# Gate scores of a dense mixture: tokens as the stationary operand of 96 small matmuls, and column sums in columns that the products leave free

## The chip, the cores and the metric

The kernel runs on one core of one Trainium2 chip. The metric is the device time of one execution in microseconds (us). The engines of a core work side by side, each through its own list of instructions, and wait for each other by semaphores: TensorE (PE, with its weight loads shown as PEld), VectorE (DVE), ScalarE (ACT), GpSimd (POOL) and SyncE (SP), which issues most of the transfers (DMA).

## The reference, cut to what matters

Three stages follow one another: a decayed linear attention, a mixture of experts that sends each of the N = 1536 tokens to one of 8 experts, and a second, dense mixture in which every token passes all 8 experts. The change lies in the gate of the dense mixture:

```
logits = x @ w_gate                  # x: 1536 x 512, w_gate: 512 x 8
logits = logits - logits.max()       # one maximum over all tokens and experts
P = np.exp(logits)
for _ in range(8):
    P /= P.sum(1, keepdims=True) + 1e-09
    P /= P.sum(0, keepdims=True) + 1e-09
    P *= N / E
for e in range(E):
    out += P[:, e:e+1] * (np.maximum(x @ w1[e], 0.0) @ w2[e])
```

## The kernel before, in words

All matrix products of the two mixtures keep float32 accuracy by splitting an operand into a high and a low part of the type float32r: `x2T[0]` and `x2T[1]` hold the two parts of the transposed tokens of the dense mixture, `w1r` and `w2r`/`w2l` those of the weights, `hb` those of the hidden values. The helper `product` multiplies hi by hi, hi by lo and lo by hi: 12 matmuls of 384 columns for one 128 x 384 block of hidden values (lines 780 to 782 of the profile). `relu` then reads the block out of PSUM, first on ACT (L785), then on DVE (L786).

PSUM has eight banks of 512 columns. Banks 0 to 5 collect the output of six blocks of 128 tokens. Banks 6 and 7, called `pa` and `pc`, take the products in turn; a product uses columns 0 to 383 of its bank.

The dense mixture goes through its work in groups, and the order of the instructions is written out by hand. Group 0 is `opening`: four products (z = 0 to 3) with nothing between them. It stands in both branches of a condition on the number of slots of the first mixture, so the instructions behind it come after a branch. Groups 1 to 3 are run by `eight(n, points)`: for each z a product, its `relu`, and three `triple`s (three matmuls of 512 columns each, L969 to L971) that use the hidden values of the group before. `points` names small functions that are called at the end of a given z of a given group. Group 4 and most later ones are run by `seven`.

The gate of the dense mixture is spread over this order. `dense_gate` writes the gate weights to `wg2s`, 8 columns of high parts and 8 of low parts; the other 112 of 128 columns hold zeros (memset, L442). Behind the branch, before group 1, come on ACT and DVE the last weight splits of the opening's expert: `conv1(7, NE)`, whose transfer of the second weights SP may issue only when the split has read the buffer, and `conv2(4)` to `conv2(7)`, of which the last needs that transfer (L297 on ACT, L298 on DVE). On PE, `gate_scores(c)` for c = 0 to 2 takes `wg2s` as the stationary operand and 512 tokens as the moving one: 24 matmuls into banks 0 to 2 (L817). ACT copies the 16 rows that matter into `lgT`, a view of the tile `snap` (L818). Then

- group 1, z = 0: `gate_exp` turns the scores and folds the two halves together with 12 float32 matmuls of 8 columns, each of which runs as two instructions (L823), and DVE copies them to `Pm` and takes a maximum (L824, L825);
- group 1, z = 1: `gate_peak`, one small matmul (L829) that waits for that maximum;
- group 1, z = 2: `gate_shift`, another small matmul (L834), the exponential and the first sums over rows;
- groups 2 and 3, each z: `balance(at)`, a matmul of `Pm` with ones (L849, 96 columns, two instructions) into columns 0 to 95 of the bank of that z, then eight short operations on DVE (L850 to L853 and L840 to L843), the last of which gives the `Pm` that the next balance needs.

POOL adds up blocks of `x2T` into `snap` for the later groups (`xwhole`, L866 to L875) and splits them (`xsplit`, L880), beginning with group 1.

Of the kernel before, what the change touches and what calls it, by code (L numbers as in the profile page):

```python
# [11 lines left out]
F32 = mybir.dt.float32  # L12
F32R = mybir.dt.float32r
BF16 = mybir.dt.bfloat16
I32 = mybir.dt.int32
AF = mybir.ActivationFunctionType
ALU = mybir.AluOpType
AX = mybir.AxisListType
# [3 lines left out]
C = 128  # L22
# [4 lines left out]
NE = 8  # L27
# [89 lines left out]
def build(tc, i, out):  # L117
# [3 lines left out]
    with ctx:  # L121
# [13 lines left out]
        onesb = base.tile([128, 128], BF16, name="onesb")  # L135
        trib = base.tile([128, 128], BF16, name="trib")
        wg2f = base.tile([128, 4, NE], F32, name="wg2f")
        wg2s = base.tile([128, 4, 128], F32R, name="wg2s")
        mb = base.tile([128, 2, NE], F32, name="mb")
        midr = base.tile([128, M, 2], I32, name="midr")  # L140
        midf = base.tile([128, M], F32, name="midf")
# [260 lines left out]
        def attention_and_routing():  # L402
            with ExitStack() as st:
# [35 lines left out]
                V.memset(zero, 0.0)  # L439
                V.memset(onesb, 1.0)  # L440
                V.memset(ohsum, 0.0)
                V.memset(wg2s.bitcast(F32), 0.0)  # L442
                V.tensor_scalar(out=flip, in0=k("iota"), scalar1=k("phi"), scalar2=None, op0=ALU.is_equal)
                for h in range(2):
                    for g in range(4):
# [199 lines left out]
        with ExitStack() as st2:  # L645
# [138 lines left out]
            def relu(h, src):  # L784
                A.activation(out=h[:, 0], in_=src, func=AF.Relu)  # L785
                V.scalar_tensor_tensor(out=h[:, 1], in0=src, scalar=0.0, in1=h[:, 0].bitcast(F32), op0=ALU.max, op1=ALU.subtract)  # L786
# [3 lines left out]
            def opening():  # L790
                for z in range(4):
                    fi, th = z % 2, z // 2
                    b = (pa, pc)[z % 2][:, 0:HT]
                    product(b, lambda t, kk: w1b[fi][:, t, kk], lambda t, kk: x2T[t][:, kk, th * HT:(th + 1) * HT], True, True, 4)
                    relu(hs[0][fi][th], b)

            with tc.If(nsv < NREST + 1) as short:
                opening()
# [8 lines left out]
            sraw = op.tile([128, 4, 256], F32, name="sraw")  # L807
            snap = op.tile([128, 4, HT], F32, name="snap")
            oacc = []
            lgT = snap.rearrange("p u t -> p (u t)")[0:2 * NE]  # L810
            rs, cs, gm = tab[:, 430:430 + M], tab[:, 446:446 + NE], tab[:, 458:460]
            ones12 = [128, M, NE]
            def gate_scores(c):
                b = bank[c]
                for t in range(2):
                    for kk in range(4):
                        T.matmul(out=b, lhsT=wg2s[:, kk], rhs=x2T[t][:, kk, c * 512:(c + 1) * 512], start=t == 0 and kk == 0, stop=t == 1 and kk == 3)  # L817
                A.activation(out=lgT[:, c * 512:(c + 1) * 512], in_=b[0:2 * NE], func=AF.Copy)  # L818

            def gate_exp():  # L820
                b = bank[5]
                for m in range(M):
                    T.matmul(out=b[:, m * NE:(m + 1) * NE], lhsT=lgT[:, m * C:(m + 1) * C], rhs=k("fold")[0:2 * NE], start=True, stop=True)  # L823
                V.tensor_copy(out=Pm, in_=b[:, 0:M * NE].rearrange("p (m e) -> p m e", e=NE))  # L824
                V.tensor_reduce(out=gm[:, 0:1], in_=Pm, axis=AX.XY, op=ALU.max)  # L825

            def gate_peak():
                b = bank[5][:, 128:256]
                T.matmul(out=b[0:1, 0:128], lhsT=gm[:, 0:1], rhs=gtab[:, 0, 0:128], start=True, stop=True)  # L829
                V.tensor_reduce(out=gm[0:1, 1:2], in_=b[0:1, 0:128], axis=AX.X, op=ALU.max)  # L830

            def gate_shift():
                b = bank[5][:, 256:257]
                T.matmul(out=b[:, 0:1], lhsT=ones[0:1], rhs=gm[0:1, 1:2], start=True, stop=True)  # L834
                V.tensor_scalar(out=Pm, in0=Pm, scalar1=b[:, 0:1], scalar2=None, op0=ALU.subtract)
                A.activation(out=Pm, in_=Pm, func=AF.Exp)
                balance_rows()
# [7 lines left out]
            left = [ITERS]  # L845

            def balance(at):
                b = at[:, 0:M * NE]
                T.matmul(out=b, lhsT=ones, rhs=Pm.rearrange("p m e -> p (m e)"), start=True, stop=True)  # L849
                V.tensor_reduce(out=cs, in_=b.rearrange("p (m e) -> p e m", e=NE), axis=AX.X, op=ALU.add)  # L850
                V.tensor_scalar(out=cs, in0=cs, scalar1=1e-9, scalar2=None, op0=ALU.add)
                V.reciprocal(out=cs, in_=cs)
                V.scalar_tensor_tensor(out=Pm, in0=Pm, scalar=float(N) / NE, in1=bc(cs, 1, ones12), op0=ALU.mult, op1=ALU.mult)  # L853
                left[0] -= 1
                if left[0]:
                    balance_rows()
# [122 lines left out]
            def eight(n, points):  # L979
# [9 lines left out]
                for z, (fi, th) in enumerate(((0, 0), (1, 0), (0, 1), (1, 1))):  # L989
# [1 line left out]
                    h = hs[n][fi][th] = spare.pop(0)  # L991
                    product(b, w[fi], lambda t, kk, th=th: x2T[t][:, kk, (2 * p + th) * HT:(2 * p + th + 1) * HT], True, True, 4)
                    relu(h, b)
                    for _ in range(3):
                        for fn in (next(todo, None),):
                            if fn:
                                fn()
                    if old and z in (1, 3):
                        spare.extend((old[0][z // 2], old[1][z // 2]))
                    if z == 0:  # L1000
# [63 lines left out]
            points = {  # L1064
                1: {0: [gate_exp], 1: [gate_peak], 2: [gate_shift]},
            }
            for n in range(2, 4):
                points[n] = {z: [lambda z=z: left[0] and balance((pa, pc)[z % 2])] for z in range(4)}
            for j, at, lag in ((0, 1, 2), (1, 32, 0)):
                for kk in range(2):  # L1070
                    for z, fn in ((lag, lambda j=j, kk=kk: xwhole(j, kk)), (lag + 3 - lag // 2, lambda kk=kk: xsplit(kk))):
# [5 lines left out]
            load_w(5, 0)  # L1077
            load_w(4, 1)
            load_w(5, 1)
            for c in range(3):  # L1080
                gate_scores(c)
            for n in range(1, len(groups)):
                kind = groups[n][2]
                if kind == "seven":
# [24 lines left out]
```

## Time and profile before

| | |
|---|---|
| Median of 3 runs | 1261.62 us (1259.93 to 1261.7) |
| Profiled execution, device time | 1260.48 us |
| Its span, first to last instruction | 1258.7 us |
| Mean granted TensorE clock | 0.998 of 2.4 GHz |
| PE busy, weight loads busy | 1246.2 us (99%), 1133.8 us (90%) |
| DVE, ACT, POOL busy | 678.4, 490.9, 423.3 us |

The profiled execution has a time of its own, 1.8 us longer than its span. A busy PE is not PE at its peak: matmuls overlap in the pipeline, so what one costs is read from the distance between two starts, not from its duration.

### The profile page before, as it was taken

To read this page: it belongs to the slowest core of one execution; us is meant where nothing else is said; L and a number is where in the kernel's file an instruction comes from. 1 tells how busy PE (TensorE), PEld (TensorE's weight loads), DVE (VectorE), ACT (ScalarE), POOL (GpSimd) and SP (SyncE) were. 2 spreads that over 40 slices of the span, in tenths; PEclk is the share of its full clock that TensorE was granted. 3 is DMA by queue.
4 is the path that set the end of the run, shared out by engine and by line. 5 is a ranking of instruction groups with operands and counts; after the bars stand their busy time and mean duration, and the time that the engine had idled before them with its cause. 6 is when DMAs were issued, how large, how long until landed. Compare 5 with 4: busy or idle time off the path is not lost.

```text
span 1258.7 us, 19258 instructions
## 1 busy us (share of the span) xinstructions
PE 1246.2 (99%) x7284; PEld 1133.8 (90%) x7284; DVE 678.4 (54%) x1319; ACT 490.9 (39%) x981; POOL 423.3 (34%) x411
## 2 busy tenths in 40 slices
PE   8999999999999999999999999999999999999998
PEld 7899999889999999999999999999999999999996
DVE  7787777346545454545454546354545454545453
ACT  2344555313333333444444433343333333333331
POOL 5401010153333333333333347133333333333332
PEclk9999999999999999999999999999999999999999
DMA  8933655301222222222222232122222222222201
GB/s 311 303 115 121 209 183 160 112 1 42 68 67 68 67 68 67 67 67 67 68 68 67 67 101 85 58 68 71 68 70 68 67 65 71 67 67 68 67 26 51
DMA packets 56841, 112.47 MB, mean 89 GB/s; under 512 B 7088, under 2 KB 7344, under 8 KB 56736
## 3 DMA queue, kind: packets, MB, share of 16 engines
q1 hardware_dynamic: 52272, 100.89, 26.1%
q0 software_dynamic: 2304, 7.05, 1.7%
q10 hardware_dynamic: 2160, 3.18, 0.7%
q8 instruction: 60, 0.98, 0.3%
q14 instruction: 45, 0.37, 0.1%
HBM read 104.80 MB, written 6.29 MB: 88 GB/s over the span
## 4 chain that ended last, share of the span: by engine, by line
PE 96%; DVE 1%; DMA 1%; POOL 1%; issue 1%; ACT 0%; POOLq 0%; SPq 0%; DVEq 0%; ACTq 0%
PE banks L971 14%; PE banks L970 14%; PE banks L969 14%; PE banks L781 13%; PE banks L780 13%; PE banks L782 13%; PE banks L327 2%; PE banks L329 2%; PE banks L328 2%; PE banks L657 2%; PE banks L656 2%; PE banks L658 2%; PE banks L524 1%; PE banks L398 1%; PE banks L473 1%; PE banks L503 1%
## 5 line engine op out<-in xcount | busy, mean ns | idle before, releaser
L933 POOL TENSOR_TENSOR w1r<-sraw,w1r 128x1024 fp32r<-128x1024 f32 x56 | 134.5, 2401 | 573.8 <-ACT w1r L932 573.8
L971 PE MATMUL banks<-w2r,hb 128*128 128x512 f32 x750 | 294.8, 393 | 0.0
L970 PE MATMUL banks<-w2r,hb 128*128 128x512 f32 x750 | 294.1, 392 | 0.0
L969 PE MATMUL banks<-w2r,hb 128*128 128x512 f32 x750 | 291.6, 389 | 0.0
L971 PEld LDWEIGHTS banks<-w2r,hb 128*128 128x128 f32 x750 | 140.7, 188 | 29.6
L785 ACT ACTIVATE hb<-snap 128x384 fp32r<-128x384 f32 x168 | 87.8, 523 | 201.8 <-DVE snap L1055 120.1
L780 PE MATMUL banks<-x2T,w1r 128*128 128x384 f32 x464 | 158.1, 341 | 0.0
L970 PEld LDWEIGHTS banks<-w2r,hb 128*128 128x128 f32 x750 | 140.6, 188 | 19.3
L781 PE MATMUL banks<-x2T,w1r 128*128 128x384 f32 x464 | 157.9, 340 | 0.0
L969 PEld LDWEIGHTS banks<-w2r,hb 128*128 128x128 f32 x750 | 140.8, 188 | 19.0
L782 PE MATMUL banks<-x2T,w1r 128*128 128x384 f32 x464 | 156.6, 337 | 0.0
L782 PE MATMUL banks<-xt,w1r 128*128 128x384 f32 x448 | 151.1, 337 | 0.0
L780 PE MATMUL banks<-xt,w1r 128*128 128x384 f32 x448 | 150.8, 337 | 0.0
L781 PE MATMUL banks<-xt,w1r 128*128 128x384 f32 x448 | 150.8, 337 | 0.0
L786 DVE SCALAR_TENSOR_TENSOR hb<-snap,hb 128x384 fp32r<-128x384 f32 x168 | 102.7, 611 | 66.4 <-ACT hb L785 66.4
L786 DVE SCALAR_TENSOR_TENSOR hb<-banks,hb 128x384 fp32r<-128x384 f32 x88 | 49.0, 556 | 158.7 <-ACT hb L785 158.7
L785 ACT ACTIVATE hb<-banks 128x384 fp32r<-128x384 f32 x88 | 43.3, 492 | 211.4 <-PE banks L782 209.6
L298 DVE TENSOR_TENSOR w2r<-stg,w2r 128x512 fp32r<-128x512 f32 x150 | 103.4, 691 | 4.8 <-ACT w2r L297 4.7
L297 ACT ACTIVATE w2r<-stg 128x512 fp32r<-128x512 f32 x150 | 93.2, 623 | 3.4 <-DMA stg<-in_w_dram 3.4
L781 PEld LDWEIGHTS banks<-x2T,w1r 128*128 128x128 f32 x464 | 87.3, 188 | 5.5
L780 PEld LDWEIGHTS banks<-x2T,w1r 128*128 128x128 f32 x464 | 87.3, 188 | 5.5 <-issue 0.2
L781 PEld LDWEIGHTS banks<-xt,w1r 128*128 128x128 f32 x448 | 84.1, 188 | 7.3
(228 smaller groups left out, 2086.5 us busy)
## 6 DMA issues: line engine op xcount, KB each, us to landing
stg<-in_w_dram SPq DMA_DIRECT2D x333, 256.0 KB, 2.7
pk<-in_pack_dram SPq DMA_DIRECT2D x24, 512.0 KB, 6.6
xs<-xr ACTq DMA_DIRECT2D x12, 256.0 KB, 5.8
xrow<-in_w_dram SPq DMA_DIRECT2D x3, 256.0 KB, 5.6
xrow<-xs,gidx POOLq DMA_INDIRECT x21, 3.7
out_dram<-oacc,tokmap POOLq DMA_INDIRECT x12, 2.7
cst<-in_cst_dram SPq DMA_DIRECT2D x1, 109.0 KB, 7.6
pre<-in_pre_dram SPq DMA_DIRECT2D x1, 71.0 KB, 1.9
```

The lines of the kernel that those rows point to most:

```text
L297: A.activation(out=dst[:, 0], in_=src, func=AF.Copy)
L298: eng.tensor_tensor(out=dst[:, 1], in0=src, in1=dst[:, 0].bitcast(F32), op=ALU.subtract)
L327: T.matmul(out=b, lhsT=w[:, 0, kk], rhs=xhl(0, kk), start=kk == 0, stop=False)
L780: T.matmul(out=b, lhsT=w(0, kk), rhs=x(0, kk), start=start and kk == 0, stop=False, skip_group_check=True)
L781: T.matmul(out=b, lhsT=w(0, kk), rhs=x(1, kk), start=False, stop=False, skip_group_check=True)
L782: T.matmul(out=b, lhsT=w(1, kk), rhs=x(0, kk), start=False, stop=stop and kk == kks - 1, skip_group_check=True)
L785: A.activation(out=h[:, 0], in_=src, func=AF.Relu)
L786: V.scalar_tensor_tensor(out=h[:, 1], in0=src, scalar=0.0, in1=h[:, 0].bitcast(F32), op0=ALU.max, op1=ALU.subtract)
L933: G.tensor_tensor(out=ws[:, 1], in0=sraw, in1=ws[:, 0].bitcast(F32), op=ALU.subtract)
L969: T.matmul(out=bank[mi], lhsT=h[:, 0, tok], rhs=w[:, 0], start=first, stop=False, skip_group_check=True)
L970: T.matmul(out=bank[mi], lhsT=h[:, 0, tok], rhs=w[:, 1], start=False, stop=False, skip_group_check=True)
L971: T.matmul(out=bank[mi], lhsT=h[:, 1, tok], rhs=w[:, 0], start=False, stop=last, skip_group_check=True)
```

## The change

`gate_scores` now takes one block of 128 tokens (m = 0 to 11). The tokens are the stationary operand and the 16 columns of `wg2s` the moving one, so that the scores come out with tokens on partitions, 16 columns of bank 5 for each block. Eight matmuls make one block, 96 make all, and they stand in `opening`: three blocks, 24 matmuls, behind each of its four products. The 24 matmuls of 512 columns behind the branch, the three copies on ACT and the 12 folding matmuls go away; `gate_exp` is a reduction on DVE that adds the two halves straight from PSUM. `lgT` and the zeros of `wg2s` are no longer needed. The small matmuls of `gate_peak` and `gate_shift` move to other columns of bank 5.

`balance` writes columns 384 to 479 of the other product bank, which no product touches, and is called behind the first of the three triples instead of behind the third and the rest of that z.

```diff
-        wg2s = base.tile([128, 4, 128], F32R, name="wg2s")
+        wg2s = base.tile([128, 4, 2 * NE], F32R, name="wg2s")
...
-                V.memset(wg2s.bitcast(F32), 0.0)
...
                     relu(hs[0][fi][th], b)
+                    for m in range(3 * z, 3 * z + 3):
+                        gate_scores(m)
+
+            def gate_scores(m):
+                at = bank[5][:, m * 2 * NE:(m + 1) * 2 * NE]
+                for t in range(2):
+                    for kk in range(4):
+                        T.matmul(out=at, lhsT=x2T[t][:, kk, m * C:(m + 1) * C], rhs=wg2s[:, kk], start=t == 0 and kk == 0, stop=t == 1 and kk == 3, skip_group_check=True)
...
-            def gate_scores(c):
-                b = bank[c]
-                for t in range(2):
-                    for kk in range(4):
-                        T.matmul(out=b, lhsT=wg2s[:, kk], rhs=x2T[t][:, kk, c * 512:(c + 1) * 512], start=t == 0 and kk == 0, stop=t == 1 and kk == 3)
-                A.activation(out=lgT[:, c * 512:(c + 1) * 512], in_=b[0:2 * NE], func=AF.Copy)
...
             def gate_exp():
-                b = bank[5]
-                for m in range(M):
-                    T.matmul(out=b[:, m * NE:(m + 1) * NE], lhsT=lgT[:, m * C:(m + 1) * C], rhs=k("fold")[0:2 * NE], start=True, stop=True)
-                V.tensor_copy(out=Pm, in_=b[:, 0:M * NE].rearrange("p (m e) -> p m e", e=NE))
+                V.tensor_reduce(out=Pm, in_=bank[5][:, 0:2 * M * NE].rearrange("p (m t e) -> p m e t", t=2, e=NE), axis=AX.X, op=ALU.add)
                 V.tensor_reduce(out=gm[:, 0:1], in_=Pm, axis=AX.XY, op=ALU.max)
...
             def balance(at):
-                b = at[:, 0:M * NE]
+                b = at[:, HT:HT + M * NE]
...
-                    for _ in range(3):
+                    for u in range(3):
                         for fn in (next(todo, None),):
                             if fn:
                                 fn()
+                        if u == 0 and z in sums.get(n, ()):
+                            balance((pa, pc)[(z + 1) % 2])
...
-            for n in range(2, 4):
-                points[n] = {z: [lambda z=z: left[0] and balance((pa, pc)[z % 2])] for z in range(4)}
+            sums = {2: range(4), 3: range(4)}
...
-            for c in range(3):
-                gate_scores(c)
```

The lines below the added function move: `product` is L779 to L781 after the change, `relu` L784 and L785, a triple L966 to L968, the new gate matmuls L802.

On PE, at the end of the opening, there stood before the last product, the branch, the gate matmuls with 512 tokens each and the first product of group 1:

```order
L782 MATMUL banks<-x2T_938,w1r 128x384
L797 UNCONDITIONAL_BRANCH
L817 MATMUL banks<-x2T_938,wg2s 128x512 x4
L817 MATMUL banks<-x2T_939,wg2s 128x512 x4
...
L780 MATMUL banks<-x2T_938,w1r 128x384
```

There stands now the last product, the last 24 of the small matmuls (x2T_937 and x2T_938 are the high and the low part of the tokens), the branch and the product:

```order
L781 MATMUL banks<-x2T_937,w1r 128x384
L802 MATMUL banks<-wg2s,x2T_937 128x16 x4
L802 MATMUL banks<-wg2s,x2T_938 128x16 x4
...
L804 UNCONDITIONAL_BRANCH
L779 MATMUL banks<-x2T_937,w1r 128x384
```

The gate's matmuls have moved ahead of the branch, the same piece stands behind each of the three products before it, and nothing is left between the branch and group 1.

On PE, in group 1 behind the triples of z = 0, the folding matmuls stood ahead of the product of z = 1 before:

```order
L971 MATMUL banks<-w2l,hb_932 128x512
L823 MATMUL banks<-cst,snap 128x8 x12
L780 MATMUL banks<-x2T_938,w1r 128x384
```

In this place the product now follows the triples at once.

On PE, in group 2, the matmul of a balance (Pm and ones) stood behind three triples and ahead of the next product before:

```order
L969 MATMUL banks<-w2r,hb_937 128x512
L970 MATMUL banks<-w2r,hb_937 128x512
L971 MATMUL banks<-w2r,hb_937 128x512
L849 MATMUL banks<-Pm,ones 128x96
L780 MATMUL banks<-x2T_938,w1r 128x384
```

It stands now behind the first triple, with two more triples between it and the next product:

```order
L966 MATMUL banks<-w2r,hb_936 128x512
L967 MATMUL banks<-w2r,hb_936 128x512
L968 MATMUL banks<-w2r,hb_936 128x512
L846 MATMUL banks<-Pm,ones 128x96
L966 MATMUL banks<-w2l,hb_935 128x512
```

The matmul has moved two triples, six matmuls of 512 columns, towards the front. Its eight operations on DVE follow the relu of the same z as before, and it no longer writes columns that this relu reads.

## Rows read from the trace of the kernel before

**Rows 1.** The page, part 1: busy us, share of the span, instructions.

```profile
PE 1246.2 (99%) x7284; PEld 1133.8 (90%) x7284; DVE 678.4 (54%) x1319; ACT 490.9 (39%) x981; POOL 423.3 (34%) x411
```

**Rows 2.** Timeline of PE, opening to gate_peak: start us, duration us, instructions [idle before].

```profile
226.23 0.34 PE L780 MATMUL banks<-x2T,w1r 128*128 128x384 f32 x1
...
234.49 0.34 PE L782 MATMUL banks<-x2T,w1r 128*128 128x384 f32 x1
235.50 5.85 PE L817 MATMUL banks<-x2T,wg2s 128*128 128x512 f32 x24 [0.67 <-ACT hb L785]
241.19 0.33 PE L780 MATMUL banks<-x2T,w1r 128*128 128x384 f32 x1
...
243.11 0.34 PE L782 MATMUL banks<-x2T,w1r 128*128 128x384 f32 x1
244.48 0.50 PE L969 MATMUL banks<-w2l,hb 128*128 128x512 f32 x1 [1.03 <-ACT snap L818]
...
246.77 2.84 PE L823 MATMUL banks<-cst,snap 16*128 16x8 f32 x24
249.54 0.45 PE L780 MATMUL banks<-x2T,w1r 128*128 128x384 f32 x1
...
255.50 0.38 PE L829 MATMUL banks<-gtab,tab 128*1 128x128 f32 x2
```

**Rows 3.** Lines by form: weight loads of both kinds, busy us, mean ns.

```profile
L817 PEld LDWEIGHTS banks<-x2T,wg2s 128*128 128x128 f32 x24 | 4.4, 188 | 2.0 <-ACT hb L785 1.0
L823 PEld LDWEIGHTS banks<-cst,snap 16*128 16x128 f32 x24 | 2.8, 187 | 0.4 <-issue 0.4
```

**Rows 4.** Timeline of ACT and DVE from the opening's last relu on.

```profile
234.93 0.49 ACT L785 ACTIVATE hb<-banks 128x384 fp32r<-128x384 f32 x1 [1.68 <-PE banks L782]
...
237.75 0.63 ACT L297 ACTIVATE w1r<-stg 128x512 fp32r<-128x512 f32 x1 [2.33 <-issue]
...
238.56 0.69 DVE L298 TENSOR_TENSOR w1r<-stg,w1r 128x512 fp32r<-128x512 f32 x1 [2.56 <-ACT w1r L297]
...
243.32 0.63 ACT L297 ACTIVATE w2r<-stg 128x512 fp32r<-128x512 f32 x1 [3.38 <-DMA stg<-in_w_dram]
...
245.79 0.56 DVE L786 SCALAR_TENSOR_TENSOR hb<-banks,hb 128x384 fp32r<-128x384 f32 x1 [1.11 <-ACT hb L785]
```

**Rows 5.** Timeline of POOL: first and last of the eight additions of xwhole.

```profile
247.75 1.94 POOL L866 TENSOR_TENSOR snap<-x2T,x2T 128x384 f32<-128x384 f32 x2 [56.61 <-PE banks L823]
...
254.96 1.00 POOL L875 TENSOR_TENSOR snap<-snap 128x384 f32<-128x384 f32 x1
```

**Rows 6.** Timeline of DVE: first and last operation of two balances (groups 2 and 3).

```profile
274.20 0.26 DVE L850 TENSOR_REDUCE tab<-banks 128x8 f32<-128x96 f32 x1 [0.55 <-PE banks L849]
...
277.55 0.88 DVE L843 TENSOR_TENSOR Pm<-Pm,tab 128x96 f32<-128x96 f32 x1
...
283.87 0.26 DVE L850 TENSOR_REDUCE tab<-banks 128x8 f32<-128x96 f32 x1 [0.70 <-PE banks L849]
...
285.66 0.26 DVE L843 TENSOR_TENSOR Pm<-Pm,tab 128x96 f32<-128x96 f32 x1
```

**Rows 7.** Timeline of PE: balance matmuls, and the first matmuls of the products behind them.

```profile
269.11 0.42 PE L780 MATMUL banks<-x2T,w1r 128*128 128x384 f32 x1
...
273.95 0.42 PE L780 MATMUL banks<-x2T,w1r 128*128 128x384 f32 x1
...
279.20 0.42 PE L780 MATMUL banks<-x2T,w1r 128*128 128x384 f32 x1
...
283.47 0.36 PE L849 MATMUL banks<-Pm,ones 128*128 128x96 f32 x2
283.61 0.43 PE L780 MATMUL banks<-x2T,w1r 128*128 128x384 f32 x1
```

**Rows 8.** Stages: PE busy (instructions), PEclk (granted clock), DMA share, GB/s.

```profile
246.80:249.50 2.70, 2.70 (x25) 1.00 0.44 165
...
251.00:254.00 3.00, 3.00 (x10) 0.50 0.00 0
```

More of the change, by code (lines that the diff above doesn't have):

```diff
@@ L809, in build @@
             oacc = []
-            lgT = snap.rearrange("p u t -> p (u t)")[0:2 * NE]
             rs, cs, gm = tab[:, 430:430 + M], tab[:, 446:446 + NE], tab[:, 458:460]
             ones12 = [128, M, NE]
-            def gate_scores(c):
-                b = bank[c]
-                for t in range(2):
-                    for kk in range(4):
-                        T.matmul(out=b, lhsT=wg2s[:, kk], rhs=x2T[t][:, kk, c * 512:(c + 1) * 512], start=t == 0 and kk == 0, stop=t == 1 and kk == 3)
-                A.activation(out=lgT[:, c * 512:(c + 1) * 512], in_=b[0:2 * NE], func=AF.Copy)
             def gate_exp():
-                b = bank[5]
-                for m in range(M):
-                    T.matmul(out=b[:, m * NE:(m + 1) * NE], lhsT=lgT[:, m * C:(m + 1) * C], rhs=k("fold")[0:2 * NE], start=True, stop=True)
-                V.tensor_copy(out=Pm, in_=b[:, 0:M * NE].rearrange("p (m e) -> p m e", e=NE))
+                V.tensor_reduce(out=Pm, in_=bank[5][:, 0:2 * M * NE].rearrange("p (m t e) -> p m e t", t=2, e=NE), axis=AX.X, op=ALU.add)
                 V.tensor_reduce(out=gm[:, 0:1], in_=Pm, axis=AX.XY, op=ALU.max)
             def gate_peak():
-                b = bank[5][:, 128:256]
+                b = bank[5][:, 256:384]
                 T.matmul(out=b[0:1, 0:128], lhsT=gm[:, 0:1], rhs=gtab[:, 0, 0:128], start=True, stop=True)
@@ L832, in gate_shift @@
             def gate_shift():
-                b = bank[5][:, 256:257]
+                b = bank[5][:, 384:385]
                 T.matmul(out=b[:, 0:1], lhsT=ones[0:1], rhs=gm[0:1, 1:2], start=True, stop=True)
```

## The prediction

> **What bounds the kernel now.** I read the page first: PE is busy for 99% of the span and its weight loads for 90% [rows 1], so the other engines count only where PE waits for them or where its clock is low. The change touches two stretches, the opening with group 1 and the balances of groups 2 and 3, so I took the timeline of PE through both, then that of ACT, DVE and POOL beside them, and last the granted clock by stage.
>
> From the opening's first matmul to `gate_peak` PE takes 29.27 us, 226.23 to 255.50 [rows 2]. The pieces, by distances between starts: four products 8.44 (47 steps of 0.176 to 234.49, and one more); a wait of 0.83 to 235.50, ended by ACT's last relu (0.49 from 234.93 on [rows 4]); 24 gate matmuls 5.69 (0.237 each); the product of z = 0 2.10; a wait of 1.19 to 244.48, ended by the first copy of scores on ACT; three triples 2.29; the fold 2.77; the product of z = 1 and its triples 5.96. These last 21 matmuls would take 12 x 0.176 + 9 x 0.237 = 4.24 us at the usual steps. The other 1.7 us are the clock: it was granted in full during the fold, and at 0.50, the 1.2 GHz level, from 251 to 254 [rows 8]. What the engine did before the fall were 24 instructions of 8 columns in 2.77 us and about a microsecond of product.
>
> In the balances the distance between the products of successive z is 4.84, 5.25 and 4.41 us [rows 7]. The last is what PE's work needs, so 0.43 + 0.84 = 1.27 us are waiting. Nearly all of it is DVE's: one balance takes from 274.20 to 278.43 while POOL adds beside it, and 283.87 to 285.92, half of that, when POOL is silent [rows 6].
>
> **The change, part by part.** *Removed on PE*: 5.69 us of gate matmuls, 2.77 of fold, the waits of 0.83 and 1.19, and the 1.7 us that the low clock took. Together 12.2 us.
>
> *Added on PE*: 96 matmuls of 16 columns, each with a new stationary operand of 128 rows and 128 columns. No row shows such a matmul. The nearest is the fold: 24 instructions with 8 columns and a new load each, 2.77 us, 0.115 each [rows 2]. Its loads have 16 rows, but a load of 128 rows lasts just as long, 188 against 187 ns [rows 3]. So I take 96 x 0.115 = 11.1 us. Entering the fold cost 2.29 - 9 x 0.237 = 0.16, four times 0.6. From below: the two instructions of a balance matmul let the next product start 0.14 us after the first, 0.07 each [rows 7]; but the second reloads the same ones, and a wide matmul ahead hides the first load. From above: loads that nothing overlaps, 0.188 each, 18.0 us. I take 11.7 in all.
>
> The Trainium skill, "TensorE: Matmul & The Clock Gate", section "LDWEIGHTS (loading the stationary operand)", has a load cost its columns at 1.2 GHz whatever its rows. The trace agrees on the rows: 187 and 188 ns [rows 3]. By the page's figure a load of 128 columns is 107 ns, and my estimate from it for 96 is 10.2 us, which would make the sum 0.9 us lower; the rule speaks against the change, since few columns in the moving operand save nothing below that.
>
> *Where PE is then at `gate_peak`*: 226.23 + 8.44 + 11.7 + 0.2 for the branch (between 0 and the 0.83 of now; the last relu is done beside the last 24 small matmuls) + two products with triples, 2 x 4.24 = 8.5, gives 255.1.
>
> *What else `gate_peak` needs* is the maximum on DVE. Ahead of it in ACT's and DVE's order stand the last splits behind the branch. `conv1(7)` on ACT starts 2.82 us after the last relu, DVE's half frees the buffer at 239.25, and the transfer that SP issues then lets `conv2(7)` begin on ACT at 243.32 [rows 4]. This chain starts with the opening's last relu, which now comes three stretches of 2.93 us, 8.8 us, later: `conv2(7)` at 252.1, DVE's half (0.69) from 252.8 to 253.5, relu (0.56) to 254.0, two reductions of about 0.3 (the 0.26 of rows 6, with twice the elements in one) to 254.6. POOL adds to it: its eight additions, 247.75 to 255.96, began when the fold had read `snap` [rows 5]. Now nothing holds them but the end of the opening, near 246.5, so they run beside the splits. In rows 6 they doubled eight operations, 0.27 us each; for two splits and the relu I take 0.6 us, at most 1.2 (one addition is 1.0). So DVE is ready at 255.2, 254.6 to 255.8. `gate_peak` starts at 255.2 instead of 255.50: a gain of 0.3 us, between a gain of 0.4 and a loss of 0.3.
>
> *Balances*: the matmul no longer waits for the relu of its own z, and it is asked for two triples earlier. What remains is a circle of 4.23 on DVE beside POOL plus 0.40 from matmul to DVE (283.47 to 283.87) [rows 6, 7], 4.63 against PE's 4.41: 0.2 in each of two quarters. I take 0.8 of the 1.27 us as gained, between 0 (if relu and balance only change places in the queue of DVE, where the next relu waits behind the eight operations) and 1.27. Behind the waiting matmul two triples and the next product are queued, and no engine waits for these but through them.
>
> *At nothing*: three copies on ACT, which then has only the relu to do while PE runs the product and triples of z = 0; the memset, one DVE operation while the first inputs arrive, at most the 0.69 of a split of the same size [rows 4] if that cover were gone; the moved columns of `gate_peak` and `gate_shift`.
>
> Without the clock the sum is 0.3 + 0.8 = 1.1 us gained, 1259.4 us on the profiled execution's 1260.48.
>
> **The clock.** The fold was one stretch of 24 small instructions, and a loss of 1.7 us followed. The change issues four, each as long, with only 2.1 us of product between them. A fall may begin inside a stretch and slow its loads too; I price each at the 1.7 us of the one that is seen. Not each stretch must draw one: the waiting around 234.49 and 243.29 drew none. I count three, 5.1 us, between two (3.4) and five (8.5).
>
> **The rivals.** *A, three falls of the clock*: 1260.48 - 1.1 + 5.1 = 1264.5 us; with two 1262.8, with five 1267.9. For it speaks rows 8; against it that the fold filled only 16 rows of the array and came after a wait of 1.19 us.
>
> *B, none or one*: 1259.4 or 1261.1 us, no difference to be measured. The new stretches never leave the array without a matmul, and use all its rows. The same page of the Trainium skill, "Why this matters for your kernels", names gaps without matmuls as what takes the clock down; by that rule there is no fall here and the time is B's 1259.4. The trace does not quite agree: PE's longest gap before the fall was 1.19 us and had been over for 6 us, and the fold lay between.
>
> *C, faster*: the loads are hidden better than in the fold. At 0.07 each PE saves 96 x 0.045 = 4.3 us and the chain over ACT and DVE 72 x 0.045 = 3.2, so `gate_peak` starts 3.2 earlier: 1256.2 us. It decides from 0.095 us for a small matmul on (72 x 0.02 = 1.4 us, with 1.1 makes 2.5). Against it stand 24 starts at 0.115.
>
> *D, slower by the loads*: 0.188 each, 7.0 us more, 1266.4 us without any fall. Against it: the fold's loads last 0.187 and still start every 0.115.
>
> **How the numbers follow.** A 0.52, B 0.30, C 0.12, D 0.06. A bound of 0.2%, 2.5 us, is about what a measurement of this kernel tells from no change. Slower are A with three falls or more (0.42) and D; same are A with two (0.10) and most of B; faster C and a B with better balances: 0.14, 0.39 and 0.47. The profiled execution lies 1.1 us under the median of the three runs, 1261.62, and these lie 1.8 apart, about one fall of the clock. A is 1264.5 against the one and 1265.6 against the other; I give 1264.8. The range takes in B below and four falls, with the unknown costs, above, and leaves C out: 1259 to 1268 us. A's own range is 1262.5 to 1268.
>
> **What would show it.** In the profile after: 24 small matmuls in 2.77 us wherever the clock is full (2.3 or less is C, 4 or more D); a clock of 0.50 in or just behind at least two of the four stretches (none is B); `gate_peak` at 255.2 plus 1.7 for each fall, with PE arriving last or within half a microsecond of DVE; POOL's additions beginning at the end of the opening; quarters of 4.4 to 4.7 us in groups 2 and 3. I am wrong if the clock stays full, if the small matmuls cost another price than the fold's, or if time comes from outside these 75 us.

## The result, and the profile after

The changed kernel takes 1269.95 us (median of 6 executions, 1266.65 to 1271.84), the kernel before 1261.66 (1259.55 to 1264.24): 1.0063 times as long, with an interval of 1.0042 to 1.0084. I had given 1264.8 us and a range of 1259 to 1268. The direction was right; the time lies above the range.

The profiled execution of the changed kernel takes 1268.8 us, and its span is 1267.0. On its page PE has 48 instructions more than in [rows 1] (96 new ones, 24 + 24 gone) and is busy for ten microseconds more:

```profile
PE 1255.9 (99%) x7332; PEld 1145.4 (90%) x7332; DVE 680.0 (54%) x1318; ACT 489.5 (39%) x978; POOL 423.5 (33%) x411
```

The timeline of PE from the opening to `gate_peak` answers to [rows 2] (start us, duration us, instructions):

```profile
228.11 0.34 PE L779 MATMUL banks<-x2T,w1r 128*128 128x384 f32 x1
...
230.21 2.74 PE L802 MATMUL banks<-wg2s,x2T 128*128 128x16 f32 x24
...
236.54 2.74 PE L802 MATMUL banks<-wg2s,x2T 128*128 128x16 f32 x24
...
242.48 3.14 PE L802 MATMUL banks<-wg2s,x2T 128*128 128x16 f32 x24
...
248.41 5.12 PE L802 MATMUL banks<-wg2s,x2T 128*128 128x16 f32 x24
253.38 0.67 PE L779 MATMUL banks<-x2T,w1r 128*128 128x384 f32 x1
...
263.58 0.38 PE L826 MATMUL banks<-gtab,tab 128*1 128x128 f32 x2
```

`gate_peak` starts 35.47 us behind the opening's first matmul; before it was 29.27. (The opening itself begins 1.9 us later. Nothing was changed ahead of it, and all experiments below have its start between 227.7 and 228.4, e1 and e6 with the opening of before among them: in this it is the profiled execution of the kernel before that stands apart. So of the 8.3 us between the two profiled executions 6.2 lie here and 1.9 ahead of the opening.) The first stretch of 24 small matmuls lets the next product start 2.60 us after it, 0.108 each. The fourth takes 4.97 us, 0.207 each. None of the rows carries a wait: PE works without a gap shown and falls 6.2 us behind. The table by stretches shows why (PE, PEld, DVE, ACT, POOL busy, then the granted clock, DMA share, GB/s):

```profile
233.10:236.40 3.30, 3.30 (x12) 3.30 (x11) 0.00 (x0) 0.00 (x0) 3.14 (x4) 0.50 0.01 2
236.60:239.00 2.40, 2.40 (x24) 2.40 (x23) 0.56 (x1) 0.49 (x1) 2.31 (x3) 1.00 0.00 0
240.00:243.30 3.30, 3.30 (x14) 3.30 (x12) 0.06 (x1) 0.49 (x1) 0.08 (x1) 0.50 0.00 0
243.40:245.40 2.00, 2.00 (x20) 2.00 (x20) 0.40 (x1) 0.00 (x0) 0.00 (x0) 1.00 0.00 0
...
248.50:253.30 4.80, 4.80 (x25) 4.80 (x23) 1.56 (x3) 2.39 (x5) 0.00 (x0) 0.50 0.04 10
253.50:256.90 3.40, 3.40 (x12) 3.40 (x12) 1.29 (x3) 0.09 (x1) 0.00 (x0) 0.50 0.56 162
257.00:263.00 6.00, 6.00 (x30) 5.33 (x30) 2.24 (x5) 1.51 (x3) 0.00 (x0) 1.00 0.93 297
```

The clock is at 0.50, the 1.2 GHz level, three times: 233.07 to 236.49, 239.90 to 243.31 and 246.73 to 256.97, by the places where the steps between matmuls change from 0.176 to 0.32 us and back. That is 17.07 us. By the steps of the full clock (0.176, and 2.60 for a stretch) the same instructions would have taken about 7.8 us less: 1.5 and 1.6 us are lost in the first two falls and 4.7 in the third. The first two falls begin less than a microsecond behind a stretch of small matmuls, as I had thought. The third begins 1.3 us behind the third stretch, and then the fourth stretch runs in it from end to end, and nearly all of group 1's first product after that.

The other rows answer to [rows 3] (loads in the first stretch), [rows 4] (ACT, then DVE) and [rows 5]:

```profile
L802 PEld LDWEIGHTS banks<-wg2s,x2T 128*128 128x128 f32 x24 | 2.8, 192 | 0.0
```

```profile
251.40 0.63 ACT L297 ACTIVATE w1r<-stg 128x512 fp32r<-128x512 f32 x1 [2.20 <-issue]
...
257.46 0.63 ACT L297 ACTIVATE w2r<-stg 128x512 fp32r<-128x512 f32 x1 [3.87 <-DMA stg<-in_w_dram]
...
259.58 0.25 DVE L822 TENSOR_REDUCE tab<-Pm 128x1 f32<-128x96 f32 x1
```

```profile
231.88 1.96 POOL L863 TENSOR_TENSOR snap<-x2T,x2T 128x384 f32<-128x384 f32 x2 [38.85 <-DVE hb L785]
...
239.07 1.01 POOL L872 TENSOR_TENSOR snap<-snap 128x384 f32<-128x384 f32 x1
```

The maximum on DVE is ready at 259.83, 3.75 us before PE reaches `gate_peak`, so the chain of splits does not bind. POOL's additions run inside the opening, not beside the splits: what held them is, by the profile, the DVE half of the first relu.

In the balances, the first matmuls of the products and the one balance that waits answer to [rows 7], and a chain on DVE beside POOL to [rows 6]:

```profile
272.92 0.33 PE L779 MATMUL banks<-x2T,w1r 128*128 128x384 f32 x1
...
277.31 0.34 PE L779 MATMUL banks<-x2T,w1r 128*128 128x384 f32 x1
...
282.09 0.34 PE L779 MATMUL banks<-x2T,w1r 128*128 128x384 f32 x1
...
285.51 0.46 PE L846 MATMUL banks<-Pm,ones 128*128 128x96 f32 x2 [0.47 <-DVE Pm L840]
287.22 0.34 PE L779 MATMUL banks<-x2T,w1r 128*128 128x384 f32 x1
...
291.62 0.34 PE L779 MATMUL banks<-x2T,w1r 128*128 128x384 f32 x1
```

```profile
280.87 0.26 DVE L847 TENSOR_REDUCE tab<-banks 128x8 f32<-128x96 f32 x1
281.16 1.05 DVE L848 TENSOR_SCALAR tab<-tab 128x8 f32<-128x8 f32 x1
...
284.59 0.86 DVE L840 TENSOR_TENSOR Pm<-Pm,tab 128x96 f32<-128x96 f32 x1
```

The quarters are 4.39, 4.78, 5.13 and 4.40 us. These rows begin one quarter (one z) earlier than [rows 7], so the last three answer to 4.84, 5.25 and 4.41: 0.06, 0.12 and 0.01 us are gained. One balance beside POOL now takes 4.58 us (280.87 to 285.45), 0.35 more than before, and the matmul waits for its result instead of for the relu.

**Where the time went.** Every execution comes with its span and its mean granted clock. The span times what the clock lacks of 1 is about what the execution lost to a low clock; the rest of its time is what it would take at the full one. (The clock is given to 0.001, 1.3 us of one execution, and the loss is counted a little high: a step of a product grows from 0.176 to 0.32 us, not to 0.352. It also holds a low clock at the very end, where PE has little to do: in e1 the clock is at 0.86 from 1250 us to the end at 1259, with PE busy for 2.9 us of the nine.) Means over the executions of each kernel, with the experiments below; the ratio is to the kernel before on the same chip:

| kernel | median us (n) | ratio, interval | lost to the clock | rest |
|---|---|---|---|---|
| before | 1261.6 (65) | 1 | 2.3 | 1259.1 |
| after | 1269.95 (6) | 1.0063, 1.0042 to 1.0084 | 10.6 | 1259.0 |
| e1 balances alone | 1262.0 (11) | 1.0002, 0.9993 to 1.0011 | 2.9 | 1259.0 |
| e2 gate alone | 1270.49 (6) | 1.0059, 1.0044 to 1.0074 | 9.7 | 1260.0 |
| e3 wide | 1264.35 (11) | 1.0019, 1.001 to 1.0027 | 2.8 | 1261.5 |
| e4 dealt, 6 6 6 6 | 1263.85 (11) | 1.0018, 1.0009 to 1.0026 | 3.1 | 1260.7 |
| e5 dealt, tail of 12 | 1263.9 (11) | 1.0014, 1.0005 to 1.0023 | 2.9 | 1260.8 |
| e6 before, fold dealt | 1262.33 (12) | 1.0009, 0.9999 to 1.0019 | 3.1 | 1259.6 |
| e7 last 24 dealt | 1268.86 (4) | 1.0052, 1.0037 to 1.0066 | 10.1 | 1259.1 |
| e8 first 72 dealt | 1264.64 (10) | 1.0026, 1.0017 to 1.0035 | 3.8 | 1261.0 |
| e9 dealt, 8 8 8 0 | 1272.85 (4) | 1.0095, 1.0078 to 1.0111 | 13.0 | 1259.6 |
| e10 24 behind the branch | 1266.76 (4) | 1.0046, 1.0029 to 1.0062 | 6.0 | 1260.8 |

Between before and after the rest stands still, 1259.1 and 1259.0, and the loss to the clock grows by some 8 us. Within what this count can tell, that is all of the slowdown.

### The profile page after: what moved, and what is told of

Same layout as the page of the kernel before. It is cut to its first block, busy times and chain, and to the rows that moved or that the text cites. A ratio compares the mean times of both kernels' runs of the same rounds, so it can differ in the third digit from the quotient of the medians.

```text
span 1267.0 us, 19346 instructions
## 1 busy us (share of the span) xinstructions
PE 1255.9 (99%) x7332; PEld 1145.4 (90%) x7332; DVE 680.0 (54%) x1318; ACT 489.5 (39%) x978; POOL 423.5 (33%) x411
## 4 chain that ended last, share of the span: by engine, by line
PE 96%; DVE 2%; DMA 0%; issue 0%; POOL 0%; ACT 0%; another core or an unknown queue 0%; POOLq 0%; SPq 0%; ACTq 0%; DVEq 0%
PE banks L968 14%; PE banks L967 14%; PE banks L966 13%; PE banks L779 13%; PE banks L780 13%; PE banks L781 13%; PE banks L327 2%; PE banks L329 2%; PE banks L328 2%; PE banks L656 2%; PE banks L655 2%; PE banks L657 2%; PE banks L398 1%; PE banks L802 1%; PE banks L523 1%; PE banks L472 1%
## 5 line engine op out<-in xcount | busy, mean ns | idle before, releaser
L968 PE MATMUL banks<-w2r,hb 128*128 128x512 f32 x750 | 294.8, 393 | 0.0
L966 PE MATMUL banks<-w2r,hb 128*128 128x512 f32 x750 | 292.1, 390 | 0.0
L968 PEld LDWEIGHTS banks<-w2r,hb 128*128 128x128 f32 x750 | 140.7, 188 | 29.6
L784 ACT ACTIVATE hb<-snap 128x384 fp32r<-128x384 f32 x168 | 87.8, 523 | 200.5 <-DVE snap L1054 120.1
L780 PE MATMUL banks<-x2T,w1r 128*128 128x384 f32 x464 | 159.9, 345 | 0.0
L779 PE MATMUL banks<-x2T,w1r 128*128 128x384 f32 x464 | 159.6, 344 | 0.1
L781 PE MATMUL banks<-x2T,w1r 128*128 128x384 f32 x464 | 158.3, 341 | 0.0
L966 PEld LDWEIGHTS banks<-w2r,hb 128*128 128x128 f32 x750 | 140.8, 188 | 18.8
L781 PE MATMUL banks<-xt,w1r 128*128 128x384 f32 x448 | 151.1, 337 | 0.0
L779 PE MATMUL banks<-xt,w1r 128*128 128x384 f32 x448 | 150.8, 337 | 0.0
L785 DVE SCALAR_TENSOR_TENSOR hb<-banks,hb 128x384 fp32r<-128x384 f32 x88 | 49.0, 557 | 171.8 <-ACT hb L784 171.8
L785 DVE SCALAR_TENSOR_TENSOR hb<-snap,hb 128x384 fp32r<-128x384 f32 x168 | 103.0, 613 | 66.4 <-ACT hb L784 66.4
L784 ACT ACTIVATE hb<-banks 128x384 fp32r<-128x384 f32 x88 | 43.3, 492 | 218.5 <-PE banks L781 211.3
L779 PEld LDWEIGHTS banks<-x2T,w1r 128*128 128x128 f32 x464 | 88.5, 191 | 6.3 <-DVE tab L847 0.5
```

The lines of the kernel that those rows point to most:

```text
L779: T.matmul(out=b, lhsT=w(0, kk), rhs=x(0, kk), start=start and kk == 0, stop=False, skip_group_check=True)
L780: T.matmul(out=b, lhsT=w(0, kk), rhs=x(1, kk), start=False, stop=False, skip_group_check=True)
L781: T.matmul(out=b, lhsT=w(1, kk), rhs=x(0, kk), start=False, stop=stop and kk == kks - 1, skip_group_check=True)
L966: T.matmul(out=bank[mi], lhsT=h[:, 0, tok], rhs=w[:, 0], start=first, stop=False, skip_group_check=True)
L968: T.matmul(out=bank[mi], lhsT=h[:, 1, tok], rhs=w[:, 0], start=False, stop=last, skip_group_check=True)
```

## The experiments

The theory was A: the stretches of small matmuls take the clock down. Against it stood the loads themselves (C and D), the balances, and the rule that only gaps do it (B).

**e1, the balances alone**: the kernel before with this part of the change.

```diff
-                b = at[:, 0:M * NE]
+                b = at[:, HT:HT + M * NE]
...
+                        if u == 0 and z in sums.get(n, ()):
+                            balance((pa, pc)[(z + 1) % 2])
...
-                points[n] = {z: [lambda z=z: left[0] and balance((pa, pc)[z % 2])] for z in range(4)}
```

> The kernel before with the balances alone changed: column sums in columns 384 to 479 of the other bank, called behind the first triple. Theory A (the clock falls in the stretches of small matmuls and that is the whole loss): nothing of it is here, so the time is within 0.5 us of before, and groups 2 and 3 take as long as in the kernel after, 36.7 us against 36.4 before. Rival B (the balances were mispriced and carry a part of the loss, since group 3 now has its weight split behind the eight operations): 1 to 2 us slower than before. The prediction had 0.8 us faster.

Measured 1262.0 us, no difference. The four quarters of groups 2 and 3 gave nothing; the loss is not here. The trace holds a second answer, the clock over the whole opening and group 1 (window), and the fold, still in one stretch (timeline of PE):

```profile
228.00:260.00 32.00, 30.89 (x166) 27.09 (x164) 9.02 (x18) 8.19 (x17) 7.93 (x8) 1.00 0.28 86
```

```profile
248.32 2.84 PE L823 MATMUL banks<-cst,snap 16*128 16x8 f32 x24
```

The same fold as in [rows 2] draws no fall here, with the same instructions ahead of it. So the fall in [rows 8] does not come every time; the mean clock of the kernel before, 0.996 to 0.999 from one execution to another, fits that.

**e2, the gate alone**: the changed kernel with the balances of the kernel before (e1's edits taken back).

```diff
-                b = at[:, HT:HT + M * NE]
+                b = at[:, 0:M * NE]
...
-                        if u == 0 and z in sums.get(n, ()):
-                            balance((pa, pc)[(z + 1) % 2])
```

> The kernel after with the balances of before: the 96 small matmuls in the opening, nothing else. Theory A: all of the loss is here, 1269 to 1270 us, with the clock at 0.50 for some 14 to 17 us in and behind the opening. Rival B (a part of the loss lies in the balances): 1 to 2 us faster than the kernel after, 1268 us.

Measured 1270.49 us, all of the loss. With e1 this puts the slowdown into the gate's matmuls. In the profile three falls stand again, but not in the same places. They last about 10, 3.4 and 7 us, more than the 14 to 17 us expected, and the long one now begins in the second product (windows):

```profile
234.00:244.00 10.00, 10.00 (x41) 10.00 (x41) 0.56 (x1) 0.49 (x1) 5.80 (x6) 0.50 0.00 0
247.60:250.80 3.20, 3.20 (x11) 3.20 (x11) 0.00 (x0) 0.00 (x0) 0.00 (x0) 0.50 0.00 0
254.50:261.00 6.50, 5.50 (x16) 5.21 (x17) 3.74 (x7) 2.87 (x6) 0.00 (x0) 0.50 0.60 192
```

The opening is the same as in the changed kernel. So where the falls begin and how long each one lasts differs from execution to execution; here the fourth stretch ran at full clock, and PE waited 1.90 us behind the branch, up to 255.50.

**e3, wide**: the changed kernel with 128 columns in the moving operand, of which 112 hold zeros.

```diff
-        wg2s = base.tile([128, 4, 2 * NE], F32R, name="wg2s")
+        wg2s = base.tile([128, 4, 128], F32R, name="wg2s")
...
-                at = bank[5][:, m * 2 * NE:(m + 1) * 2 * NE]
+                at = bank[5][:, m * 2 * NE:m * 2 * NE + 128]
```

> The kernel after with a moving operand of 128 columns in the 96 matmuls (16 of weights, 112 of zeros, so the scores are the same): the loads stay the same, 96 x 0.108 = 10.4 us, and 128 columns stream in about 128 x 0.46 = 59 ns, inside a load. Theory A (the clock falls because few columns pass through the array): no fall in the opening, 8.5 us less than the kernel after, about 1261 us. Rival C (the clock stays low whenever the weights change this often, however many columns pass): the same falls and 1270 us. Rival D (the loss is the loads themselves, the clock is by the way): 1270 us or more.

Measured 1264.35 us. The 96 loads are the same and in the same places, a stretch takes 2.63 us instead of 2.60 (229.90 to 232.53), and the opening keeps its clock:

```profile
228.00:246.80 18.80, 18.80 (x144) 18.80 (x142) 2.80 (x6) 2.36 (x5) 7.93 (x8) 1.00 0.04 15
```

So eight times the columns cost 0.001 us a matmul and save 5.6 us. Loads at a price of their own (D) would have stayed. The 3.3 us that are missing to the 1261 expected lie behind the branch: PE waits there for 1.92 us, and the clock falls within this wait and stays at 0.50 for close to 7 us:

```profile
249.50:254.50 5.00, 5.00 (x16) 4.71 (x15) 2.53 (x5) 1.14 (x3) 0.00 (x0) 0.50 0.79 271
```

No matmul of 16 columns stands ahead of this fall, so they are not the only thing that goes before one; what draws it stays open. The profile puts the wait down to the split of `w1r` on DVE, but that split fills the eighth weight buffer, which this product does not read, and in e4 the same product starts 2.4 us before the split does (248.51 against 250.93). What PE waits for is not shown; e2, e5 and e8 have such a wait too.

**e4, dealt out**: the same 96 matmuls of 16 columns, six behind each three matmuls of a product.

```diff
-                    product(b, lambda t, kk: w1b[fi][:, t, kk], lambda t, kk: x2T[t][:, kk, th * HT:(th + 1) * HT], True, True, 4)
...
-                    for m in range(3 * z, 3 * z + 3):
-                        gate_scores(m)
+                    for kk in range(4):
+                        T.matmul(out=b, lhsT=w(0, kk), rhs=x(0, kk), start=kk == 0, stop=False, skip_group_check=True)
+                        T.matmul(out=b, lhsT=w(0, kk), rhs=x(1, kk), start=False, stop=False, skip_group_check=True)
+                        T.matmul(out=b, lhsT=w(1, kk), rhs=x(0, kk), start=False, stop=kk == 3, skip_group_check=True)
...
+                        for _ in range(6):
+                            next(small)
```

> The kernel after with the same 96 small matmuls dealt out evenly: six behind each three matmuls of an opening product, instead of 24 behind twelve. The work is the same. Theory A in the form that a long stretch of small matmuls brings the clock down: no fall, about 1261 us. Theory A in the form that the mean of columns over the opening is too low: falls as before, 1268 to 1272 us. Rival D (the loads themselves): 1270 us with either clock.

Measured 1263.85 us. The windows show the opening at full clock and a fall behind the branch, and the timeline the wait there:

```profile
228.50:247.40 18.90, 18.90 (x145) 18.90 (x143) 2.33 (x5) 2.15 (x5) 7.89 (x8) 1.00 0.04 15
249.00:252.00 3.00, 3.00 (x11) 3.00 (x10) 1.07 (x2) 2.01 (x4) 0.00 (x0) 0.50 0.04 14
```

```profile
248.51 0.51 PE L779 MATMUL banks<-x2T,w1r 128*128 128x384 f32 x1 [0.93 <-DVE hb L785]
```

The same instructions in another order are 6.1 us faster. Changes of the stationary operand are now spread over the whole opening, so it is not their number, nor the mean of columns over the whole opening, which is the same.

**e5, e4 with a tail**: the fourth product gets 4, 4, 4 and 12 instead of four times 6.

```diff
-                        for _ in range(6):
+                        for _ in range(6 if z < 3 else (4, 4, 4, 12)[kk]):
```

> As the kernel of e4 (1263.85 us, 2.1 above before), with the last 24 small matmuls dealt out 4, 4, 4 and 12 behind the three-matmul steps of the fourth product, so that 12 of them cover the last relu. Theory 1 (the fall that e4 still shows, 248.77 to 252.18, comes from the 0.93 us that PE waits behind the branch): no wait, no fall there, a gain of 0.9 + 1.7 = 2.6 us on e4, 1261.2 us, the same as before. Theory 2 (it comes from the small matmuls ahead of it): the wait goes, the fall stays, a gain of 0.9 us, 1262.9 us.

Measured 1263.9 us, as e4, which is neither theory's number alone. The profiled execution has no fall at all up to `gate_peak`, but a longer wait behind the branch:

```profile
246.15 1.40 PE L809 MATMUL banks<-wg2s,x2T 128*128 128x16 f32 x12
249.12 0.44 PE L779 MATMUL banks<-x2T,w1r 128*128 128x384 f32 x1 [1.57 <-issue]
```

```profile
249.20:257.50 8.30, 8.30 (x42) 7.42 (x42) 4.74 (x9) 3.70 (x7) 0.00 (x0) 1.00 0.67 224
```

Over all executions the loss to the clock is 2.9 us, against e4's 3.1, so what draws e4's last fall stays open. The wait did not go, though the last relu was done: both theories were wrong there.

**e6, the fold dealt out**: the kernel before, with four folding matmuls behind each of the three triples.

```diff
-                for m in range(M):
-                    T.matmul(out=b[:, m * NE:(m + 1) * NE], lhsT=lgT[:, m * C:(m + 1) * C], rhs=k("fold")[0:2 * NE], start=True, stop=True)
...
+                        if n == 1 and z == 0:
+                            for m in range(4 * u, 4 * u + 4):
+                                T.matmul(out=bank[5][:, m * NE:(m + 1) * NE], lhsT=lgT[:, m * C:(m + 1) * C], rhs=k("fold")[0:2 * NE], start=True, stop=True)
```

> The kernel before, with its 12 folding matmuls dealt out four behind each of the three triples of group 1, z = 0, and nothing else changed. Theory (a stretch of small matmuls takes the clock down, dealt out it does not): no clock of 0.50 behind the fold, 1.7 us gained less 0.3 for two more entries, 1.4 us, 1260.3 us against 1261.75. Rival (the fall comes from something else near it, the waits of 0.67 and 1.03 us or the end of the opening): the clock still falls, 1262.0 us.

Measured 1262.33 us, the rival. The window behind it:

```profile
251.70:254.70 3.00, 3.00 (x11) 3.00 (x10) 0.03 (x1) 0.00 (x0) 2.84 (x4) 0.50 0.00 0
```

The fall is there without the one stretch, and in e1 the stretch is there without the fall. This does not clear the fold: its 24 small instructions still stand ahead of the fall, eight behind each three wide matmuls, as many behind three as in e9 below. What is shown is that the 1.7 us that I booked as a gain do not hang on the unbroken stretch and do not come in every execution.

**e7 and e8, one stretch and three**: e7 keeps the first three stretches and deals out the last 24, e8 deals out the first 72 and keeps the last stretch (first and second new line, against e4).

```diff
-                        for _ in range(6):
+                        for _ in range(6 if z == 3 else 24 * (kk == 3)):
...
+                        for _ in range(6 if z < 3 else 24 * (kk == 3)):
```

> The kernel after, with its first three stretches of 24 as they are and the last 24 small matmuls dealt out six behind each three-matmul step of the fourth product. Theory (each stretch draws a fall of some 3.4 us, and the fourth stretch keeps the clock low for three times as long): three falls of 3.4 us, 5.1 us lost in place of 8.5, with a wait of 0.9 us at the branch 2.5 us less than after, 1267.4 us. Rival (the third fall would last 10 us whatever follows it): no gain, 1270 to 1271 us.

> The kernel after, with the first 72 small matmuls dealt out six behind each three-matmul step of the first three products and the last 24 in one stretch behind the fourth. Theory (a stretch draws one fall of 3.4 us behind it, priced at 1.7 us): no fall before the fourth stretch, none of its loads at half clock, no wait at the branch, one fall in group 1: 1261.75 - 0.6 (gate_peak at full clock 26.9 us behind the opening's start in place of 27.6) + 1.7 - 1.7 (before's own fall) = 1261.2 us. Rival (what lies behind the branch holds the clock low, however the 72 are placed): a fall of 7 to 10 us, 3.5 to 5 us lost, 1263 to 1264.5 us.

e7 measured 1268.86 us, e8 1264.64. Windows of e7, the third stretch and then the fourth product with its pieces of six:

```profile
242.00:247.00 5.00, 5.00 (x26) 5.00 (x24) 0.56 (x1) 0.49 (x1) 0.00 (x0) 0.50 0.00 0
247.00:256.00 9.00, 9.00 (x38) 9.00 (x37) 0.42 (x1) 0.49 (x1) 0.00 (x0) 0.50 0.01 4
```

Here the clock was low from about 240.5 to 260.9, behind one short fall (233.6 to 237.0). The pieces of six, which in e4 left the full clock alone, did not bring a low one back. The median lies between the two forecasts and the four executions, 1267.19 to 1271.96, cover both; the profiled one is the slowest. But its fall of 20 us is longer than either forecast had it, and over the four executions the loss to the clock, 10.1 us, is hardly less than the changed kernel's 10.6. So it is not the fourth stretch by its form that keeps a fall long. e8's last stretch ran at full clock, and one fall followed it in group 1 (249.73 to 253.04), as the theory had it; but PE then waited behind the branch. Its time is nearer to the rival's, but not by the rival's long fall. Of the 3.4 us that e8 costs over the 1261.2 expected, that wait is half; 1.5 are what it loses to the clock beyond the kernel before:

```profile
244.60 2.74 PE L809 MATMUL banks<-wg2s,x2T 128*128 128x16 f32 x24
249.07 0.44 PE L779 MATMUL banks<-x2T,w1r 128*128 128x384 f32 x1 [1.72 <-issue]
```

**e9 and e10, none ahead of the branch**: e9 puts eight behind each three matmuls of the first three products and none into the fourth; e10 keeps six in the first three and moves the last 24 into group 1's first product, six behind each three matmuls (against e4, e9's new line first).

```diff
-                        for _ in range(6):
+                        for _ in range(8 if z < 3 else 0):
...
+                        for _ in range(6 if z < 3 else 0):
...
+                    if n == 1 and z == 0:
+                        small = gate_scores(range(9, 12))
```

> As the kernel of e4, with all 96 small matmuls dealt out in the first three products, eight behind each step of three matmuls, and none behind the fourth. In e5 and e8, with 12 and 24 small matmuls just ahead of the branch, PE stood 1.57 and 1.72 us behind it with nothing shown that it waited for; in the kernel before, with a product ahead of it, 0.67 us. Theory 1 (the last relu or what stands just ahead of the branch sets this wait): 0.7 to 0.9 us of wait, without the clock's share 0.7 us less than e5 and e8, some 1263.2 us. Theory 2 (the crossing costs PE 1.6 us or more whenever its next work is a product of group 1): a wait of 1.6 us or longer, 1263.9 us or more. The clock should stay full in the opening in both.

> As the kernel of e4, with the last 24 small matmuls moved behind the branch, six behind each step of three matmuls of group 1's first product. Theory 1 (the wait at the branch is a fixed delay after the last product's relu, as in the kernel before): 0.7 to 0.9 us of wait, 1263 us. Theory 2 (1.6 us of crossing, whatever lies ahead): a wait of 1.6 us or longer, 1264 us. In both the clock stays full in the opening, and the loss to the clock over all runs stays near the 2.4 to 3 us of before and e4.

e9 measured 1272.85 us, the slowest of all, where both theories had counted on a full clock. Its windows, and one of its pieces with the next product step:

```profile
228.00:234.70 6.70, 6.70 (x55) 6.70 (x53) 1.06 (x3) 0.82 (x2) 0.53 (x1) 1.00 0.10 36
234.80:258.40 23.60, 23.60 (x94) 23.60 (x94) 1.43 (x3) 1.47 (x3) 7.20 (x8) 0.50 0.00 1
```

```profile
251.72 1.71 PE L809 MATMUL banks<-wg2s,x2T 128*128 128x16 f32 x8
253.28 0.67 PE L796 MATMUL banks<-x2T,w1r 128*128 128x384 f32 x1
```

Eight small matmuls in place of six behind the same three, and the clock is at half for 23.6 us in which PE and its loads are busy without a gap. This is the clearest case for A: between e4 and e9 nothing changes but how closely the same small matmuls follow one another (and that the fourth product, which e9 runs at half clock too, has none). On the wait behind the branch e9 says nothing: PE comes there late and does not wait.

e10 measured 1266.76 us, 2.8 us more than the higher of the two forecasts. The opening keeps its clock, but the loss over all executions is 6.0 us, where 2.4 to 3 were expected. Behind the branch PE waits 0.84 us and, after eleven small matmuls, 0.66 more, and the clock then falls:

```profile
245.46 0.79 PE L1001 MATMUL banks<-x2T,w1r 128*128 128x384 f32 x3 [0.84 <-issue]
...
248.56 0.17 PE L809 MATMUL banks<-wg2s,x2T 128*128 128x16 f32 x1 [0.66 <-issue]
```

The first wait is theory 1's and the two together nearly theory 2's, so e10 does not decide between them either. No version here beats the kernel before.

## Why the prediction was wrong

**The mechanism was A, and it was right.** The same 96 matmuls made wider (e3) or dealt out by six (e4) keep the clock in the opening; set closer (e9) they lose it. The likeliest case and its sign came as given. That there were three falls is in part luck: in e2 the same opening has three as well, but other ones, and e7, with three of the four stretches, has two.

**The step that failed is the price of the clock**: "I count three, 5.1 us" at 1.7 us each. Three there were, but they lasted 3.42, 3.41 and 10.24 us and cost 1.5, 1.6 and 4.7 us, 7.8 together. The price held for the short falls and failed for the long one. I had written that a fall may slow the loads inside a stretch and still priced each like the one in [rows 8], where usual matmuls follow. Here the next stretch follows, and in e7 and e9 narrow matmuls that meet a low clock leave it low. Five falls, my upper case, would have been 8.5 us; what came was nearly that much in three.

**The base of that sum was a single execution.** I credited the removal of the fold with the 1.7 us of its fall, and e1 shows the fold without that fall. The kernel before loses 2.3 us to the clock on average; e1 and e6 with the fold lose 2.9 and 3.1, e3, e4 and e5 without it 2.8 to 3.1. So taking the fold away gave nothing that can be seen. The 2.7 us that the falls were priced too low, these 1.7 and the gain from the balances that did not come make about 5 us, which is what lies between 1264.8 and 1269.95.

**B**, none or one fall, is out. It rested on there being no gap, as does the section "Why this matters for your kernels" of the Trainium skill's page "TensorE: Matmul & The Clock Gate". The trace does not agree: 0.50 over 23.6 us of PE with no gap shown in e9. That page's "LDWEIGHTS (loading the stationary operand)" does agree: 107 ns by its figure for 128 columns, 0.108 us measured where the clock is full.

**C and D** are out by the same 0.108 us. C decided below 0.095; the price of 0.115 was 0.007 too high, 0.7 us over 96.

**PE at `gate_peak`.** At full clock I had 28.9 us behind the opening's start (255.1 less 226.23). e5's profile, with no fall, has 29.34 (228.34 to 257.68): the small matmuls take 10.8 us in all instead of 11.7, and the wait behind the branch, which I set at 0.2, is 1.57. In the profile of the changed kernel this wait does not appear; its fourth stretch ran 2.4 us longer than at full clock, while in e2, where that stretch ran at full clock, PE waits for 1.90.

**The chain over ACT and DVE** was ready 3.75 us early, where I had it last by 0.1. (At full clock in the opening it is early too: in e5 the maximum is ready at 256.04 and PE starts `gate_peak` at 257.68. Only in e9 does PE wait for it, 0.60 us.) POOL's collisions with the splits, 0.6 us in my sum, did not take place: the additions had the first relu for a start, not the end of the opening.

**Balances**: 0.8 us of gain became 0.2 in the profile and none that could be measured (e1, 1.0002). It was near the lower bound that I had named: the circle on DVE beside POOL grew from 4.23 to 4.58 us, and the wait moved from the relu to the balance's own matmul. The longest quarter, 5.13 us, lies outside the 4.4 to 4.7 that I gave as a sign.

**The chances** do not add up as written: A with three falls or more and D are 0.42 and 0.06, which makes 0.48 for slower and not 0.47.

## What to carry to other kernels

A matmul of few columns with a new 128-column load costs the load, and a run of such matmuls can also cost the clock of everything that stands near it: here 0.108 us each by themselves, and 8 us in 17 of low clock for their neighbourhood. Where such work must be done, the wide form (tokens moving, or columns filled up with zeros, 0.001 us more each) is worth its columns, and dealing it out between wide matmuls has to be measured, since six held and eight did not. Price the clock from many executions and not from the one that was profiled, and split a comparison into the loss to the clock and the rest before looking for waits.

## What was not expected of the hardware

- A low clock held for as long as the narrow work went on and a few microseconds longer, 20 us in e7 and 23.6 in e9, with PE busy throughout.
- Pieces of six small matmuls behind three of 384 columns keep a full clock (e4, 18.9 us) and do not lift a low one (e7, 9 us).
- Where PE comes to the branch at full clock right behind 12 or 24 small matmuls, it stands 1.57 to 1.90 us (e5, e8, e2) with nothing shown that it waits for. ACT stands 2.20 to 2.85 us at the same place in all profiles, the one before (2.33, [rows 4]) among them. What this time is, stays open.
- One `TENSOR_SCALAR` of 8 columns on DVE took 1.05 us beside POOL's additions and 0.17 (286.30, L848) a few microseconds later, with an addition of POOL's (285.42 to 286.43) still on the timeline. So POOL at work does not by itself make it long.
